# Two f tiles at a time on TensorE, and attention scores as 64x64 matmuls in its quadrants

## The chip, the cores and the metric

The kernel runs on one core of a Trainium2 chip. The metric is the device time of one execution in microseconds (us), as a median of several runs. Lower is better. TensorE multiplies matrices, VectorE (DVE), ScalarE (ACT) and GpSimd (POOL) work on elements, and SyncE (SP) issues the DMA transfers. PSUM is the memory that TensorE writes to.

## The reference

Local attention with block summaries, and then a feed-forward layer with a squared relu. There are 4 batches, 8 heads, 768 tokens and 64 channels per head. Each query sees the keys less than 16 positions away, and one summary key for each of 24 blocks of 32 tokens (the maximum over the block; the mean for the values).

```python
k_sum = k.reshape(B, H, nb, block, D).max(axis=3)
v_sum = v.reshape(B, H, nb, block, D).mean(axis=3)
scores_l = np.where(mask_l, scale * (q @ k.T), -1e9)       # |i - j| < 16
scores_s = scale * einsum('bhsd,bhnd->bhsn', q, k_sum) + log(block)
a = softmax(concatenate([scores_l, scores_s], axis=-1))
x = (a @ concatenate([v, v_sum], axis=2)).reshape(B * S, H * D)   # 3072 x 512
h = np.maximum(x @ w_in, 0.0)                              # 512 -> 2048
out = h * h @ w_out                                        # 2048 -> 512
```

All arrays are float32. The products are made of high and low parts, so each layer of the feed-forward part takes three products instead of one.

## The kernel before, in words

**Tiles.** The 3072 tokens are 24 query tiles g of 128 (t = g % 6 is a tile's place in its batch). A tile has two halves s of 64 queries; a half sees 96 keys of its window and 24 block keys, 120 columns in all (NK). Two tiles make a chunk c of 256 tokens, 12 chunks in all. The hidden 2048 columns are 16 f tiles of 128.

**Feed-forward, per chunk and f.** A row of the first layer (`ffn1`, L318) is 12 matmuls of 128x256 into a PSUM buffer `ph`, of which there are three in rotation. ACT then makes the relu `r` (L327) and the square `gh` (L334); DVE makes the exact square in `ph` (L339) and the rest `gl` (L343). The subtraction at L343 is the last reader of `ph` and sets its buffer free. A row of the second layer (`ffn2`, L359) is 6 matmuls of 128x512 which add to the two output buffers `o_ps` of the chunk. After f 15, `evict` copies both to SBUF on ACT (L106) and sends them out.

**Attention, per tile g.** `scores` (L222) makes 8 matmuls, one per head, into the two `s_ps` buffers of four heads each. The weights `q_sb` are 128x128: the two halves of the queries stand in two diagonal blocks of 64, and the other two blocks hold zeros, filled once by POOL (L103). `mask_max` (DVE, L234) and `exponentials` (ACT, L242) make the softmax, `inverse` and `norm` (DVE, POOL L257) divide, `turn` (L270) transposes 32x32 blocks on DVE, 12 instructions a tile, `outputs` (L283) makes 16 matmuls of 64 weight columns into `x_ps`, and `split_x` (L301, L304) splits the result into `xh` and `xl`, which `ffn1` reads. `place_k` copies the 24 block keys into `k_sb` with four copies of 64x96 on DVE (L157); for each batch after the first this is done for its first two tiles.

**The order of the work.** Every engine takes its instructions in the order in which the program records them. The start, chunks 0 and 1 and tiles 0 to 5, is a table written by hand (`START`): a token is one step, `F1.12` the first layer's row 12, `S4.1` the scores of half the heads of tile 4, `PK` the placing of the block keys. From chunk 2 on, `slot` records one f at a time: the first-layer row of f, the second-layer row of f - 2 (with the eviction after f 15), the attention's steps for this slot (`side`), relu to subtraction of f, and then what stands in `last` (scores, outputs, loads). `steps` gives each tile ten steps, and the loop at the end lays them over the slots of the chunk ahead: tile 2c + 2 is at step f + 2, tile 2c + 3 at step f - 6, tile 2c + 4 at step f - 14. So the outputs of one tile and the scores of the next but one come at the end of the same slot.

## Time and profile before

| what | value |
|---|---|
| median of 3 runs | 664.42 us (664.35 to 664.96) |
| profiled execution, its own time | 663.47 us |
| its span (first to last work on the core) | 661.7 us |
| TensorE busy | 633.0 us, 96% of the span |
| DVE, ACT, POOL busy | 404.9, 301.1, 110.6 us |
| granted TensorE clock, mean | 0.992 |
| moved by DMA | 61.87 MB, mean 94 GB/s |

The profile is one execution. A group's row shows the line, the engine, the operation, output <- inputs, the shape and the count; then the busy time, the mean ns of one, and the idle time ahead of it with what ended it. A timeline row shows start (us), length (us), engine, line and operation; `x2` joins two of a kind, and an idle time ahead of it stands in brackets. A row of busy time by stretches shows busy us of PE, PEld (weight loading), DVE, ACT and POOL with their counts, the granted clock, the DMA share and GB/s. A float32 matmul has two records in the trace. Starts of matmuls are measured, their lengths are modelled and overlap, so paces are read from start to start.

### The profile page before, as it was taken

Reading aid. Unit: us, or ns where it says so; the run is one execution under the profiler, and the core shown is the slowest. Engines: PE = TensorE matmul, PEld = TensorE weight load, DVE = VectorE, ACT = ScalarE, POOL = GpSimd, SP = SyncE. Lnnn points to the kernel's source line nnn. Section 1 sums busy time; section 2 is a strip of 40 time slices with the busy share of each in tenths; the row PEclk is TensorE's granted clock in tenths of the full one; section 3 lists DMA queues with packets and bytes.
Section 4 is the critical chain, followed back from the end, with each engine's and each line's share of the span. In section 5 each row is a group of like instructions: output and inputs, shape, how many; then the busy total and the mean of one; then the engine's idle time right before and its main releaser. Section 6 shows DMA issues by size and latency. Waiting matters only on the chain.

```text
span 661.7 us, 12338 instructions
## 1 busy us (share of the span) xinstructions
PE 633.0 (96%) x4668; PEld 566.5 (86%) x4668; DVE 404.9 (61%) x1247; ACT 301.1 (46%) x854; POOL 110.6 (17%) x87
## 2 busy tenths in 40 slices
PE   1788999999999999999999999999999999999997
PEld 1477999888889889999899998899898899988996
DVE  4678787656664684874863675865765645645332
ACT  2778867524424435335344344343444443443322
POOL 5464573401011011010010010010010110110000
PEclk9879999999999999999999999999999999999999
DMA  9999525005203314303103133212022020000000
GB/s 326 367 363 376 151 73 209 1 33 136 64 1 97 103 57 144 112 1 97 42 24 97 28 133 112 97 49 64 32 65 64 33 64 25 33 2 1 33 1 32
DMA packets 42314, 61.87 MB, mean 94 GB/s; under 512 B 27792, under 2 KB 27920, under 8 KB 40208
## 3 DMA queue, kind: packets, MB, share of 16 engines
q1 hardware_dynamic: 42256, 61.10, 28.3%
q8 instruction: 36, 0.59, 0.4%
q14 instruction: 22, 0.18, 0.1%
HBM read 54.80 MB, written 6.29 MB: 92 GB/s over the span
## 4 chain that ended last, share of the span: by engine, by line
PE 92%; DVE 3%; DMA 2%; ACT 1%; issue 1%; POOL 1%; SPq 0%; DVEq 0%; POOLq 0%; ACTq 0%
PE ph L318 41%; PE o_ps L359 39%; PE s_ps L222 7%; PE x_ps L283 3%; PE ph L263 1%; PE o_ps L129 1%; DMA kv<-in_kt 1%; DMA q_sb<-in_q 1%; DVE pT L270 1%; ACT e_sb L242 1%; DVE k_sb L157 0%; POOL e_sb L257 0%; DVE ksum L143 0%; POOL q_sb L103 0%; DVE ph L339 0%
## 5 line engine op out<-in xcount | busy, mean ns | idle before, releaser
L318 PE MATMUL ph<-xh,w_sb 128*128 128x256 f32 x1536 | 285.3, 284 | 0.7 <-ACT xh L301 0.7
L318 PEld LDWEIGHTS ph<-xh,w_sb 128*128 128x128 f32 x1536 | 248.3, 190 | 15.8 <-ACT xh L301 0.8
L359 PE MATMUL o_ps<-w_sb,gh 128*128 128x512 f32 x768 | 241.4, 395 | 0.0
L318 PE MATMUL ph<-xl,w_sb 128*128 128x256 f32 x768 | 217.0, 283 | 0.2 <-DVE xl L304 0.2
L339 DVE TENSOR_TENSOR ph<-ph,r 128x256 f32<-128x256 f32 x192 | 82.6, 431 | 157.1 <-ACT r L327 153.8
L327 ACT ACTIVATE r<-ph 128x256 f32<-128x256 f32 x179 | 68.2, 381 | 204.9 <-PE ph L318 203.7
L359 PE MATMUL o_ps<-w_sb,gl 128*128 128x512 f32 x384 | 151.3, 394 | 0.0
L318 PEld LDWEIGHTS ph<-xl,w_sb 128*128 128x128 f32 x768 | 145.5, 189 | 0.5 <-DVE xl L304 0.4
L359 PEld LDWEIGHTS o_ps<-w_sb,gh 128*128 128x128 f32 x768 | 131.1, 188 | 17.1
L257 POOL TENSOR_TENSOR e_sb<-e_sb,sm 128x480 f32<-128x480 f32 x42 | 41.7, 994 | 421.6 <-DVE nmx L234 360.9
L242 ACT ACTIVATE e_sb<-e_sb,nmx 128x120 f32<-128x120 f32 x192 | 73.9, 387 | 57.4 <-DVE nmx L234 57.4
L343 DVE TENSOR_TENSOR gl<-ph,gh 128x256 fp32r<-128x256 f32 x192 | 81.3, 424 | 29.7 <-ACT gh L334 7.1
L270 DVE STREAM_TRANSPOSE pT<-e_sb 32x256 f32<-32x256 f32 x216 | 94.2, 436 | 5.4 <-POOL e_sb L257 2.1
L334 ACT ACTIVATE gh<-r 128x256 fp32r<-128x256 f32 x192 | 80.4, 418 | 20.3 <-DVE r L329 7.7
L359 PEld LDWEIGHTS o_ps<-w_sb,gl 128*128 128x128 f32 x384 | 72.0, 188 | 17.1
L222 PE MATMUL s_ps<-k_sb,q_sb 128*128 128x120 f32 x384 | 51.4, 286 | 14.9 <-DVE k_sb L157 14.7
L222 PEld LDWEIGHTS s_ps<-k_sb,q_sb 128*128 128x128 f32 x384 | 46.9, 197 | 17.0 <-POOL w_sb L212 14.5
L234 DVE CUSTOM_DVE_ANT_0 e_sb<-s_ps,mask_sb 128x120 f32<-128x120 f32 x192 | 43.8, 274 | 5.3 <-PE ph L263 3.1
L205 POOL TENSOR_TENSOR w_raw<-w_raw 128x1024 int32<-128x1024 int32 x16 | 32.0, 2005 | 37.4 <-DVE w_raw L201 17.3
L242 ACT ACTIVATION_READ_ACCUMULATOR e_sb<-e_sb,nmx 128x1 f32 x192 | 36.1, 188 | 0.0
L283 PEld LDWEIGHTS x_ps<-pT,v_sb 128*64 128x64 f32 x768 | 24.4, 138 | 12.7 <-issue 9.5
L304 DVE TENSOR_TENSOR xl<-x_ps,xh 128x512 fp32r<-128x512 f32 x24 | 16.5, 688 | 27.0 <-ACT xh L301 27.0
(41 smaller groups left out, 293.0 us busy)
## 6 DMA issues: line engine op xcount, KB each, us to landing
w_raw<-in_w SPq DMA_DIRECT2D x16, 1024.0 KB, 10.7
k_sb<-in_k SPq DMA_DIRECT2D x24, 384.0 KB, 3.9
v_sb<-in_v SPq DMA_DIRECT2D x24, 384.0 KB, 3.7
kv<-in_kt SPq DMA_DIRECT2D x16, 384.0 KB, 5.3
q_sb<-in_q SPq DMA_DIRECT2D x48, 128.0 KB, 3.7
out<-ob SPq DMA_DIRECT2D x24, 256.0 KB, 2.0
kv<-in_vt SPq DMA_DIRECT2D x12, 384.0 KB, 4.9
vn<-in_v SPq DMA_DIRECT2D x2, 768.0 KB, 8.5
```

Source lines behind the costliest of these rows:

```text
L222: nc.tensor.matmul(s_ps[half][:, i, 0:NK], lhsT=q_sb[g % 2][:, h, :], rhs=k_sb[g % 2][:, :, h, :], start=True, stop=True)
L234: nc.vector.tensor_tensor_reduce(out=e_sb[:, h, 0:NK], in0=s_ps[half][:, i, 0:NK], in1=m, scale=-scale, scalar=3.0e38, op0=ALU.add, op1=AL ...
L242: nc.scalar.activation(e, e, AF.Exp, bias=nmx[half][:, i : i + 1], scale=-1.0, accum_out=sm[half][:, i : i + 1])
L257: eng.tensor_mul(out=e, in0=e, in1=sm[half].unsqueeze(2).to_broadcast([P, 4, NK]))
L270: nc.vector.transpose(out=pT[g % 2][j * 32 : j * 32 + 32, :, i * 32 : i * 32 + 32], in_=e_sb[i * 32 : i * 32 + 32, :, j * 32 : j * 32 + 32],)
L283: nc.tensor.matmul(xp[o : o + 64, h // 2, s * 64 : s * 64 + 64], lhsT=v_sb[g % 2][:, s, h * 64 : h * 64 + 64], rhs=pT[g % 2][:, h, s * 64 ...
L318: nc.tensor.matmul(ph, lhsT=w_sb[f][:, w, cc * P : (cc + 1) * P], rhs=x[c][:, cc, :], start=(n == 0), stop=(n == 3 * NC4 - 1))
L327: nc.scalar.activation(r, ph, AF.Relu)
L334: nc.scalar.activation(gh, r, AF.Square)
L339: nc.vector.tensor_mul(out=ph, in0=ph, in1=r)
L343: nc.vector.tensor_sub(out=gl, in0=ph, in1=gh.bitcast(F32))
L359: nc.tensor.matmul(o_ps[c][tt], lhsT=g_[:, ts_], rhs=w_sb[f][:, w, DM:], start=(first and n == 0), stop=(last and n == 2),)
```

## The change

- `slot` takes two f: two first-layer rows, the two second-layer rows that are waiting (with the eviction after f 15), the first half of the side work, relu to subtraction of the first f, the second half of the side work, and the same of the second f; then `last`.
- `steps` has 7 steps a tile instead of 10; the softmax is in one slot, the turns go by three. Tile 2c + 2 is at step i + 3 (i + 2 in chunk 2), tile 2c + 3 at step i - 1, tile 2c + 4 at step i - 5, where i is the number of the slot of two f. The scores of a tile come after slot 1 or 5, the outputs after slot 2 or 6.
- The scores are 4 matmuls of 64x64 weights for each of the four pairs of heads (r: head of the pair, which picks the rows; s: half of the queries, which picks the columns). `q_sb` holds no zeros any more, comes in one load instead of two, and the zero fills go. The two `s_ps` buffers become one tile of two banks, one for each r.
- `place_k` is one copy of 128x192 on DVE instead of four of 64x96.
- `xh`, `xl`, `gh` and `gl` lose the 8 spare columns (`SHIFT`); `gh` and `gl` have four buffers instead of three.
- The block sums of the next batch are loaded and made one pair of heads a tile (tiles 2 to 5), not two a tile (3 and 4).
- In `START`, `S5.1` stands some 20 tokens later, and `S6.0` behind `TT5.7`.

The core of the diff:

```diff
-SHIFT = 8
-BEHIND = 2
...
-F2.13 RE15v L:w13 SQ14 MU14 SQ15 MU15 F1.16 LO12a GL14v GL15v NR4.1 TT4.1 N4.1p S5.1 RE16a TT4.2 E4.1 TT4.3 MU16
+F2.13 RE15v L:w13 SQ14 MU14 SQ15 MU15 F1.16 LO12a GL14v GL15v NR4.1 TT4.1 N4.1p RE16a TT4.2 E4.1 TT4.3 MU16
+F1.17 SQ16 TT4.0 S5.1 E4.3 GL16v E4.2 SH12 S5.0 E4.0 RE17v AD12 F1.18 MU17 L:k7 NR4.0 L:v5 L:w15 F2.14 RE18a
...
     def load_q(g):
-        for s in range(2):
-            ps = slice(s * 64, s * 64 + 64)
-            nc.sync.dma_start(out=q_sb[g % 2][ps, :, ps], in_=q[g // NT, g % NT, ps])
+        nc.sync.dma_start(out=q_sb[g % 2], in_=q[g // NT, g % NT])
...
     def place_k(g):
-        dst = k_sb[g % 2].rearrange("a k (p two) j -> a k p two j", two=2)
-        for par in range(2):
-            for s in range(2):
-                nc.vector.tensor_copy(
-                    out=dst[s * 64 : s * 64 + 64, 4, :, par, :], in_=ksum[par * 64 : par * 64 + 64]
-                )
+        nc.vector.tensor_copy(out=k_sb[g % 2][:, 4], in_=ksum.unsqueeze(1).to_broadcast([P, 2, NPAIR, NB]))
...
-    def scores(g, half):
-        s_ps[half] = ps_s.tile([P, 4, P], F32, name="s_ps")
-        for i in range(4):
-            h = half * 4 + i
-            nc.tensor.matmul(
-                s_ps[half][:, i, 0:NK], lhsT=q_sb[g % 2][:, h, :], rhs=k_sb[g % 2][:, :, h, :], start=True, stop=True
-            )
+    def scores(g, p0, p1):
+        if g not in s_ps:
+            s_ps[g] = ps_s.tile([P, 2, NPAIR, P], F32, name="s_ps")
+        for p in range(p0, p1):
+            for r, s in ((0, 0), (1, 1), (0, 1), (1, 0)):
+                rs, ss = slice(r * 64, r * 64 + 64), slice(s * 64, s * 64 + 64)
+                nc.tensor.matmul(
+                    s_ps[g][ss, r, p, 0:NK], lhsT=q_sb[g % 2][rs, s, p, :], rhs=k_sb[g % 2][rs, :, s, p, :],
+                    start=True, stop=True,
+                )
...
     def high_square(r):
-        gh = shifted(CT, "gh", 3)
+        gh = work.tile([P, CT], F32R, name="gh", tag="gh", bufs=4)
...
     def slot(c, f, side, last):
-        ph = ffn1(c, f)
-        if len(behind) == BEHIND:
+        ph = [ffn1(c, f + i) for i in range(2)]
+        while behind:
             follow(*behind.pop(0))
-        for do in side:
-            do()
-        behind.append((c, f, *squares(ph), f == 0, f == NF - 1))
+        m = (len(side) + 1) // 2
+        for i in range(2):
+            for do in side[:m] if i == 0 else side[m:]:
+                do()
+            behind.append((c, f + i, *squares(ph[i]), f + i == 0, f + i == NF - 1))
         for do in last:
             do()
...
-        last[0] += [lambda: scores(g, 0), lambda: scores(g, 1)]
+        last[0].append(lambda: scores(g, 0, NPAIR))
...
-        side[1].append(lambda: softmax(g, 0, 2))
-        side[2].append(lambda: softmax(g, 2, 5))
-        side[3] += [lambda: inverse(0), lambda: norm(0, nc.gpsimd), lambda: softmax(g, 5, 8)]
-        side[4] += [lambda: inverse(1), lambda: norm(1, nc.gpsimd)]
-        for n in range(3):
-            side[5 + n].append(lambda n=n: turn(g, 4 * n, 4 * n + 4))
-        last[8].append(lambda: outputs(g))
+        side[1] += [lambda: softmax(g, 0, 5), lambda: softmax(g, 5, 8)]
+        for half in range(2):
+            side[2].append(lambda half=half: (inverse(half), norm(half, nc.gpsimd)))
+        for n in range(4):
+            side[3 + n // 2].append(lambda n=n: turn(g, 3 * n, 3 * n + 3))
+        last[5].append(lambda: outputs(g))
...
-            for f in range(NF):
+            for i in range(NF // 2):
                 side, last = [], []
-                at(side, last, 2 * c + 2, f + 2)
-                at(side, last, 2 * c + 3, f - 6)
-                at(side, last, 2 * c + 4, f - 14)
-                slot(c, f, side, last)
+                at(side, last, 2 * c + 2, i + (2 if c == 2 else 3))
+                at(side, last, 2 * c + 3, i - 1)
+                at(side, last, 2 * c + 4, i - 5)
+                slot(c, 2 * i, side, last)
```

How instructions move, at three places. First ACT where one chunk ends and chunk 5 begins, before. `r` and `gh` are relu and square, `ph` with a number is one first-layer row's buffer, `ob` is the copy of a finished output; `ph_3348` is f 0 of the new chunk, `ph_3382` f 1.

```order
L242 ACTIVATE e_sb_85,sm_3372<-e_sb_85,nmx_3371 128x120
L327 ACTIVATE r_3375<-ph_3348 128x256
L334 ACTIVATE gh_3377<-r_3375 128x256
L106 COPY ob_3401<-o_ps_2855 128x512
L106 COPY ob_3404<-o_ps_2856 128x512
L242 ACTIVATE e_sb_85,sm_3372<-e_sb_85,nmx_3371 128x120 x3
L327 ACTIVATE r_3416<-ph_3382 128x256
L334 ACTIVATE gh_3418<-r_3416 128x256
```

The same place on ACT in the changed kernel; `ph_3427` is f 0, `ph_3440` f 1, `ph_3367` and `ph_3380` are the last two f of the chunk before.

```order
L319 ACTIVATE r_3410<-ph_3367 128x256
L326 ACTIVATE gh_3412<-r_3410 128x256
L319 ACTIVATE r_3420<-ph_3380 128x256
L326 ACTIVATE gh_3422<-r_3420 128x256
L104 COPY ob_3465<-o_ps_2930 128x512
L104 COPY ob_3468<-o_ps_2931 128x512
L319 ACTIVATE r_3479<-ph_3427 128x256
L326 ACTIVATE gh_3481<-r_3479 128x256
L319 ACTIVATE r_3489<-ph_3440 128x256
```

The two copies stood between f 0 and f 1, and stand ahead of both now. On TensorE of the changed kernel, the fourth first-layer row of the chunk (f 3, the row after `ph_3496`) begins with a matmul that waits for DVE, and so do the scores that follow after the two second-layer rows:

```order
L310 MATMUL ph_3496<-xl_3116,w_sb_127 128x256
L310 MATMUL ph_3509<-xh_3114,w_sb_503 128x256 [waits DVE_49]
L310 MATMUL ph_3509<-xh_3114,w_sb_503 128x256
...
L351 MATMUL o_ps_3523<-w_sb_388,gh_3491 128x512 x2
L351 MATMUL o_ps_3523<-w_sb_388,gl_3494 128x512
L217 MATMUL s_ps_3557<-k_sb1_80,q_sb1_84 64x120 [waits DMAHW5_49,DMAHW6_49,DVE_49,PE_49]
L217 MATMUL s_ps_3557<-k_sb1_80,q_sb1_84 64x120 x15
L310 MATMUL ph_3576<-xh_3114,w_sb_201 128x256 x2
```

The scores are 16 instructions in one block here, and no outputs stand beside them. Last, DVE around the copy of the block keys for tile 13 (`k_sb1`), before: `pT0` are the turns of tile 12, the `L339` and `L343` rows multiply and subtract.

```order
L270 STREAM_TRANSPOSE pT0_86<-e_sb_85 32x8x32 x4
L339 TENSOR_TENSOR ph_3484<-ph_3484,r_3512 128x256
L343 TENSOR_TENSOR gl_3517<-ph_3484,gh_3514 128x256
L270 STREAM_TRANSPOSE pT0_86<-e_sb_85 32x8x32 x4
L339 TENSOR_TENSOR ph_3519<-ph_3519,r_3542 128x256
L343 TENSOR_TENSOR gl_3547<-ph_3519,gh_3544 128x256
L157 COPY k_sb1_80<-ksum_88 64x4x24 x4
L339 TENSOR_TENSOR ph_3549<-ph_3549,r_3572 128x256
```

And in the changed kernel, from f 0 of chunk 5 on (`L266` are the turns, `L331` and `L335` multiply and subtract, `L150` is the copy):

```order
L266 STREAM_TRANSPOSE pT0_86<-e_sb_85 32x8x32 x3
L331 TENSOR_TENSOR ph_3427<-ph_3427,r_3479 128x256
L335 TENSOR_TENSOR gl_3484<-ph_3427,gh_3481 128x256
L266 STREAM_TRANSPOSE pT0_86<-e_sb_85 32x8x32 x3
L331 TENSOR_TENSOR ph_3440<-ph_3440,r_3489 128x256
L335 TENSOR_TENSOR gl_3494<-ph_3440,gh_3491 128x256
L266 STREAM_TRANSPOSE pT0_86<-e_sb_85 32x8x32 x6
L331 TENSOR_TENSOR ph_3496<-ph_3496,r_3542 128x256
L335 TENSOR_TENSOR gl_3547<-ph_3496,gh_3544 128x256
L150 COPY k_sb1_80<-ksum_88 128x192
L331 TENSOR_TENSOR ph_3509<-ph_3509,r_3550 128x256
L335 TENSOR_TENSOR gl_3555<-ph_3509,gh_3552 128x256
```

All twelve turns and the squares of f 0 to f 2 now stand ahead of the copy within two slots of two f.

## The prediction

> **What bounds the kernel now.** I read the page first, for the share of each engine and the clock; then the busy time by stretches, for the part after the start; then the waits of TensorE; then the timeline around the places where the change moves work. The page's head, its busy line, the granted clock and the DMA row over the 40 slices:

> ```profile
> span 661.7 us, 12338 instructions
> PE 633.0 (96%) x4668; PEld 566.5 (86%) x4668; DVE 404.9 (61%) x1247; ACT 301.1 (46%) x854; POOL 110.6 (17%) x87
> ...
> PEclk9879999999999999999999999999999999999999
> DMA  9999525005203314303103133212022020000000
> ```

> TensorE is busy 96% of the span at nearly full clock. DMA is full only in the first four to five slices of 16.5 us. The stretch after the hand-ordered start:

> ```profile
> 180.00:650.00 470.00, 470.00 (x3484) 424.20 (x3483) 280.34 (x895) 190.35 (x595) 38.32 (x42) 1.00 0.18 57
> ```

> In these 470 us TensorE (the first pair of numbers) is busy for all 470.00 at a clock of 1.00: it waits for nobody. So there a us less of TensorE work is a us of time, and any wait that the change puts before TensorE is a us lost in full, since no slack is there to take it. The waits of TensorE over the whole span name one large one, which lies in the first 15 us:

> ```profile
> PE s_ps L222 <- DVE k_sb L157: 14.7, 2, 14.5
> ```

> This profiled execution took 663.47 us, the span 661.7 and 1.77 around it; the median of the three runs is 664.42 (664.35 to 664.96), so the profiled one is 0.95 below it. I sum against 663.47 and add 0.95 at the end. A difference of 0.2% (1.3 us) is about what a measurement of this kernel tells from none.

> **Pairing the f tiles.** The rows of the last chunk's start, at 615 us, give the paces and what I need further down:

> ```profile
> 615.20 1.29 ACT L106 COPY ob<-o_ps 128x512 f32<-128x512 f32 x2 [2.68 <-PE o_ps L359]
> 615.69 0.40 PE L318 MATMUL ph<-xh,w_sb 128*128 128x256 f32 x2
> ...
> 616.38 0.39 ACT L327 ACTIVATE r<-ph 128x256 f32<-128x256 f32 x1
> 616.80 0.42 ACT L334 ACTIVATE gh<-r 128x256 fp32r<-128x256 f32 x1
> 616.80 0.43 DVE L339 TENSOR_TENSOR ph<-ph,r 128x256 f32<-128x256 f32 x1 [3.71 <-ACT r L327]
> 617.11 0.63 PE L359 MATMUL o_ps<-w_sb,gh 128*128 128x512 f32 x2
> 617.36 0.42 DVE L343 TENSOR_TENSOR gl<-ph,gh 128x256 fp32r<-128x256 f32 x1
> 618.51 0.40 PE L318 MATMUL ph<-xh,w_sb 128*128 128x256 f32 x2
> ```

> A row of twelve first-layer matmuls takes 617.11 − 615.69 = 1.42 us (0.118 each), the six of the second 618.51 − 617.11 = 1.40 (0.233 each). Twelve times the spacing of two neighbours inside is the same 1.42: going from one layer to the other costs nothing now, so two rows of one and then two of the other gain nothing by themselves. Zero, and what TensorE does stays in number: 16 first and 16 second rows a chunk.

> **The scores.** Before, a tile's eight scores are full 128x128 matmuls (two passes each, 16 records), half of each weight being zeros. After, they are 16 64x64 matmuls, 32 records, four to a round. The price comes from two blocks in the timeline of TensorE, one of outputs followed by scores, one of outputs alone:

> ```profile
> 324.07 0.39 PE L359 MATMUL o_ps<-w_sb,gl 128*128 128x512 f32 x1
> 324.39 1.15 PE L283 MATMUL x_ps<-pT,v_sb 128*64 128x64 f32 x32
> 325.47 2.04 PE L222 MATMUL s_ps<-k_sb,q_sb 128*128 128x120 f32 x16
> ...
> 327.60 0.28 PE L318 MATMUL ph<-xl,w_sb 128*128 128x256 f32 x1
> ```
> ```profile
> 605.74 0.40 PE L359 MATMUL o_ps<-w_sb,gl 128*128 128x512 f32 x1
> 606.06 1.15 PE L283 MATMUL x_ps<-pT,v_sb 128*64 128x64 f32 x32
> ...
> 607.49 0.28 PE L318 MATMUL ph<-xl,w_sb 128*128 128x256 f32 x1
> ```

> From the last second-layer record to the third first-layer record it is 3.53 and 1.75 us; the same step without a block would be 0.233 + 2 × 0.118 = 0.47. So outputs with scores cost 3.06, outputs alone 1.28, and 16 score records 1.78, or 0.111 each for 120 columns. A 64-column output record should then take 0.059; 32 one after another would be 1.89, yet the block took 1.28. So the two column halves of the array do run at once: 16 pairs × 0.059 = 0.94, and 0.34 for going into and out of the split array. With four quadrants at once the scores would be 8 rounds × 0.111 + 0.34 = 1.23 instead of 1.78: −0.55, for the 17 tiles from 7 on −9.35. In the start, tiles 4, 5 and 6 go in two halves: 4 × 0.111 + 0.34 = 0.78 against 0.89, six times −0.105, −0.6. Together **−10.0**. That row halves also run at once no row shows. Bounds: without a switching cost −17, two at a time +7.8 (below).

> [...]

> **At a chunk's start: a new wait.** Now the copies of the finished chunk (2 × 0.65 us on ACT) stand behind the relu and square of the new chunk's f 0 and ahead of those of f 1. Afterwards the two last rows of the second layer come in one slot, and the copies stand ahead of relu and square of f 0. Behind them on ACT are both f of the slot. PSUM has three buffers for the first layer; the fourth row (f 3) needs the one of f 0, which the subtraction of f 0 on DVE sets free. The rows at 615 us show that very sequence, shifted by one f: a first-layer row starts at 615.69, right behind the chunk's last second-layer row; relu behind the copies at 616.38; subtraction until 617.36 + 0.42 = 617.78, that is 2.09 after 615.69. The fourth row is wanted 1.42 after 615.69, so TensorE stands 0.67 us, and a little for the signal. Ten boundaries (chunks 2 to 11) × 0.75 = **+7.5**; without the signal +6.7.

> **Placing the block keys: a second wait.** For tiles 7, 13 and 19 (second tile of a batch, in chunks 2, 5, 8) the copy of the block keys stands in slot 1 on DVE, behind turns of the tile before. The rows for its neighbours, and the ones of the place itself:

> ```profile
> 366.41 1.78 DVE L270 STREAM_TRANSPOSE pT<-e_sb 32x256 f32<-32x256 f32 x4 [0.29 <-POOL e_sb L257]
> 368.23 0.43 DVE L339 TENSOR_TENSOR ph<-ph,r 128x256 f32<-128x256 f32 x1
> 368.79 0.42 DVE L343 TENSOR_TENSOR gl<-ph,gh 128x256 fp32r<-128x256 f32 x1
> ```
> ```profile
> L157 DVE COPY k_sb<-ksum x32: 190/205/1743, 12.5 to 479.2; 64x96 f32<-64x96 f32 x32
> ```

> A turn is 1.78 / 4 = 0.445; multiplying and subtracting take 369.21 − 368.23 = 1.0. The new copy, 192 columns, lies between 0.2 (96 columns) and 0.43 (256 columns in the multiply); 0.3. Counted from the first-layer row of f 2: subtraction of f 0 ends at 2.1; three turns 3.4; f 1 4.4; six turns 7.1; f 2 8.1; copy 8.4, and the signal 8.5. TensorE has rows 2 and 3, the 0.75 of above and two second-layer rows, 1.42 × 2 + 0.75 + 2 × 1.40 = 6.4, and then wants scores. It stands 2.1 us, three times, in chunk 2 a little longer: **+6.5**. For even tiles the copy comes four slots later and no turns stand ahead of it: zero. In the kernel before, the copies have whole slots of cover: the waits show none of them after the start.

> **The start.** The chain that ended last, in its first pieces:

> ```profile
> 4.40 6.09 DMA kv<-in_kt
> ...
> 11.49 0.96 DVE ksum L143
> ...
> 12.48 1.74 DVE k_sb L157
> 14.23 0.21 DVE k_sb L157
> ...
> 14.54 3.67 PE s_ps L222 x16
> ...
> 18.22 5.74 DMA q_sb<-in_q
> ```

> Four copies, 12.48 to 14.44, become one of 0.2 to 1.74: up to −1.7, or nothing. The 3.67 us of scores become 8 rounds at the record pace there (0.229): −1.8. On the queue, q comes as 128 pieces of 2 KB instead of 1024 of 256 bytes, behind the same transfers: a gain with the sign known and no row for its size. Later steps of the start depend on weights that DMA brings at its limit, so part of it is lost again; bounds 0 and −3.5, I take the middle and a bit, **−2.2**. The two zero fills of q on POOL (1.85) lie beside DMA: zero. The signal of 14.44 to 14.54, 0.1, is the one used above.

> **Unpadded tiles.** The spare 8 columns behind the split activations and squares go. Prices of the readers:

> ```profile
> L318 PE MATMUL ph<-xh,w_sb 128*128 128x256 f32 x1536 | 285.3, 284 | 0.7 <-ACT xh L301 0.7
> L359 PE MATMUL o_ps<-w_sb,gh 128*128 128x512 f32 x768 | 241.4, 395 | 0.0
> L318 PE MATMUL ph<-xl,w_sb 128*128 128x256 f32 x768 | 217.0, 283 | 0.2 <-DVE xl L304 0.2
> L359 PE MATMUL o_ps<-w_sb,gl 128*128 128x512 f32 x384 | 151.3, 394 | 0.0
> ```

> Nothing in them tells padded from unpadded; different tiles of one kind differ by 1 ns. I take zero. 1 ns on 3456 records is 3.5 us either way, and 1% of the 192 first and 192 second rows, 192 × (1.42 + 1.40) = 541 us, is 5.4. Four instead of three buffers for the squares, fewer and larger loads and the softmax in one slot lie on engines that are 17 to 61% busy: zero, covered by two slots each.

> **Sum.** −10.0 − 2.2 + 7.5 + 6.5 = +1.8: 663.47 + 1.8 = 665.3, and on the median's footing 666.2.

> **The rivals.**
> *Two at a time* (0.11). Quadrants with the same rows might not overlap. Then 16 rounds: 16 × 0.111 + 0.34 = 2.12, +0.34 × 17 = +5.8; halves in the start 1.23 against 0.89, +2.0; the start gains 1.0 only: 664.42 + 7.8 − 1.0 + 14.0 = 685. The output rows speak against it, since there both column halves use all rows. All one after another (0.02) is 715. [...]
> *The other side: waits covered.* It is decided on DVE: if the turns wait for nothing and run before slot 1, the copy of the block keys is in time and TensorE never stands at the scores: 666.2 − 6.5 = 659.7 (0.13). If the buffer of f 0 also comes free in time, within 1.42 us of the row, all 14.0 go: 652 (0.07). For it: DVE is busy 280 of 470 us. Against it: engines keep their order, and the copies stood ahead of relu at 615 us.
> *Unpadded is slower* by 1%: 672 (0.12). *Unpadded is quicker* by 1 ns or more: 661 (0.09).

> **How the numbers follow.** My sum has 0.46, with its own range of ±4. The two outer cases, 652 and 685 or more (0.20), are left out: from 659.7 − 4 to 672 + 4, 656 to 676. Faster by over 0.2%: 0.09 of my own case, 0.12, 0.07, 0.07 = 0.35. Within: 0.13 of my own, the edges of others 0.05 = 0.18. Slower: the rest, 0.47.

> **What would show it.** Right: scores of a tile in 1.2 us of TensorE; TensorE idle some 14 us after 180 us, in ten pieces of 0.7 before the fourth row of a chunk, released by the subtraction, and three of 2 before scores, released by the block keys' copy; matmuls of 284 and 395 ns. Wrong: scores over 1.8, no idle time, or first-layer rows away from 1.42.

## The result, and the profile after

The changed kernel takes 655.64 us (median of 4 runs, 654.06 to 656.40), against 664.58 before: a ratio of 0.9862, with a 95% interval of 0.9843 to 0.9881. I had forecast 666.2, with a range of 656 to 676 and slower as the likelier side. The time lies just below the range, and the sign is wrong. The profiled execution, the fastest of the four, took 654.06.

The head of the page and the clock, after:

```profile
span 652.3 us, 13032 instructions
PE 608.9 (93%) x5052; PEld 535.2 (82%) x5052; DVE 402.2 (62%) x1223; ACT 295.4 (45%) x854; POOL 108.5 (17%) x85
...
PEclk9988999999999999999899999999999999999999
```

TensorE's busy time fell by 24.1 us (633.0 to 608.9), the span by only 9.4: TensorE now waits. First its busy time after the start, then who it waits for from 140 us on (us in all, times, longest):

```profile
180.00:640.00 460.00, 450.72 (x3717) 399.66 (x3717) 275.79 (x869) 184.18 (x587) 34.81 (x38) 1.00 0.18 58
```
```profile
PE ph L310 <- DVE gl L335: 5.9, 10, 0.6
PE s_ps L217 <- issue: 3.9, 2, 1.9
PE s_ps L217 <- DVE k_sb L150: 2.1, 1, 2.1
```

Both forecast waits are there: one at each of ten chunk starts, released by the subtraction, and three before scores. Two of these three are put down to "issue", which names no releaser; the rows below show the copy of the block keys ending 0.11 us before the scores start. This is chunk 5 on TensorE:

```profile
303.48 0.40 PE L310 MATMUL ph<-xh,w_sb 128*128 128x256 f32 x2
...
304.76 0.28 PE L310 MATMUL ph<-xl,w_sb 128*128 128x256 f32 x1
305.63 0.50 PE L310 MATMUL ph<-xh,w_sb 128*128 128x256 f32 x2 [0.60 <-DVE gl L335]
...
309.64 0.40 PE L351 MATMUL o_ps<-w_sb,gl 128*128 128x512 f32 x1
311.98 1.05 PE L217 MATMUL s_ps<-k_sb,q_sb 64*64 64x120 f32 x32 [1.94 <-issue]
312.96 0.55 PE L310 MATMUL ph<-xh,w_sb 128*128 128x256 f32 x2
```

And on ACT and DVE at the same place:

```profile
303.00 1.27 ACT L104 COPY ob<-o_ps 128x512 f32<-128x512 f32 x2 [6.72 <-PE o_ps L351]
304.17 0.39 ACT L319 ACTIVATE r<-ph 128x256 f32<-128x256 f32 x1
...
304.59 0.43 DVE L331 TENSOR_TENSOR ph<-ph,r 128x256 f32<-128x256 f32 x1 [5.11 <-ACT r L319]
305.15 0.42 DVE L335 TENSOR_TENSOR gl<-ph,gh 128x256 fp32r<-128x256 f32 x1
...
308.00 2.69 DVE L266 STREAM_TRANSPOSE pT<-e_sb 32x256 f32<-32x256 f32 x6
...
311.62 0.25 DVE L150 COPY k_sb<-ksum 128x192 f32<-128x192 f32 x1
```

Counted from the row of f 2 at 303.48, the subtraction of f 0 ends at 305.57 (2.09, as forecast), and the block keys' copy at 311.87 (8.39; forecast 8.4). The fourth row starts at 305.63 where 304.76 + 0.11 = 304.87 would do: 0.76 lost, and the profile calls 0.60 of it idle. The scores start 2.0 late.

What I had not foreseen shows in two first-layer rows in sequence without any wait, in the changed kernel:

```profile
326.92 0.40 PE L310 MATMUL ph<-xh,w_sb 128*128 128x256 f32 x2
...
329.66 0.62 PE L351 MATMUL o_ps<-w_sb,gh 128*128 128x512 f32 x2
...
332.41 0.40 PE L310 MATMUL ph<-xh,w_sb 128*128 128x256 f32 x2
```

Two first-layer rows take 2.74 us (2 × 1.42 = 2.84 before), two of the second 2.75 (2 × 1.40 = 2.80 before). The first five records of the pair still come every 0.118 us on average, all others every 0.113. The group means, 284 and 283 ns before, read 282 and 278:

```profile
L310 PE MATMUL ph<-xh,w_sb 128*128 128x256 f32 x1536 | 276.9, 282 | 6.6 <-DVE gl L335 5.9
...
L310 PE MATMUL ph<-xl,w_sb 128*128 128x256 f32 x768 | 213.7, 278 | 0.2 <-DVE xl L296 0.2
```

Two parts of the change are candidates: the missing spare columns, or two rows of a kind in sequence.

### The profile page after: what moved, and what is told of

It is laid out like the page before. It is cut to its first block, busy times and chain, and to the rows that moved or that the text cites. A ratio compares the mean times of both kernels' runs of the same rounds, so it can differ in the third digit from the quotient of the medians.

```text
span 652.3 us, 13032 instructions
## 1 busy us (share of the span) xinstructions
PE 608.9 (93%) x5052; PEld 535.2 (82%) x5052; DVE 402.2 (62%) x1223; ACT 295.4 (45%) x854; POOL 108.5 (17%) x85
## 4 chain that ended last, share of the span: by engine, by line
PE 90%; DVE 3%; ACT 2%; DMA 2%; issue 1%; SPq 0%; POOL 0%; DVEq 0%; POOLq 0%; ACTq 0%
PE ph L310 42%; PE o_ps L351 40%; PE x_ps L279 4%; PE s_ps L217 3%; DMA k_sb<-in_k 1%; DMA kv<-in_kt 1%; ACT e_sb L238 1%; PE ph L259 1%; DVE gl L335 1%; ACT w_raw L188 0%; ACT w_raw L184 0%; DVE pT L266 0%; DVE k_sb L150 0%; DVE sm L247 0%; SPq L134 0%
## 5 line engine op out<-in xcount | busy, mean ns | idle before, releaser
L310 PE MATMUL ph<-xh,w_sb 128*128 128x256 f32 x1536 | 276.9, 282 | 6.6 <-DVE gl L335 5.9
L310 PEld LDWEIGHTS ph<-xh,w_sb 128*128 128x128 f32 x1536 | 238.2, 189 | 18.7 <-DVE gl L335 7.9
L351 PE MATMUL o_ps<-w_sb,gh 128*128 128x512 f32 x768 | 238.6, 392 | 0.0
L310 PE MATMUL ph<-xl,w_sb 128*128 128x256 f32 x768 | 213.7, 278 | 0.2 <-DVE xl L296 0.2
L331 DVE TENSOR_TENSOR ph<-ph,r 128x256 f32<-128x256 f32 x192 | 82.3, 429 | 143.3 <-ACT r L319 140.4
L351 PEld LDWEIGHTS o_ps<-w_sb,gh 128*128 128x128 f32 x768 | 136.6, 188 | 24.2 <-ACT r L319 0.2
L335 DVE TENSOR_TENSOR gl<-ph,gh 128x256 fp32r<-128x256 f32 x192 | 81.3, 424 | 26.6 <-ACT gh L326 5.3
L266 DVE STREAM_TRANSPOSE pT<-e_sb 32x256 f32<-32x256 f32 x216 | 94.2, 436 | 4.7 <-POOL e_sb L253 0.7
L217 PE MATMUL s_ps<-k_sb,q_sb 64*64 64x120 f32 x768 | 27.3, 281 | 23.4 <-DVE k_sb L150 16.2
L217 PEld LDWEIGHTS s_ps<-k_sb,q_sb 64*64 64x64 f32 x768 | 21.2, 140 | 31.5 <-DVE k_sb L150 16.6
L104 ACT COPY ob<-o_ps 128x512 f32<-128x512 f32 x22 | 12.9, 588 | 66.2 <-PE o_ps L351 65.2
```

The costliest lines, as they stand in the source:

```text
L217: nc.tensor.matmul(s_ps[g][ss, r, p, 0:NK], lhsT=q_sb[g % 2][rs, s, p, :], rhs=k_sb[g % 2][rs, :, s, p, :], start=True, stop=True,)
L266: nc.vector.transpose(out=pT[g % 2][j * 32 : j * 32 + 32, :, i * 32 : i * 32 + 32], in_=e_sb[i * 32 : i * 32 + 32, :, j * 32 : j * 32 + 32],)
L310: nc.tensor.matmul(ph, lhsT=w_sb[f][:, w, cc * P : (cc + 1) * P], rhs=x[c][:, cc, :], start=(n == 0), stop=(n == 3 * NC4 - 1))
L331: nc.vector.tensor_mul(out=ph, in0=ph, in1=r)
L335: nc.vector.tensor_sub(out=gl, in0=ph, in1=gh.bitcast(F32))
L351: nc.tensor.matmul(o_ps[c][tt], lhsT=g_[:, ts_], rhs=w_sb[f][:, w, DM:], start=(first and n == 0), stop=(last and n == 2),)
```

## The experiments

The ratios are to the kernel before, in runs on the same chip. Differences in us between experiments sometimes cross chips; the kernel before has medians of 663.57 to 664.18 in the runs beside them.

### Spare columns or pairs: e1 and e2

The changed kernel with the spare columns put back:

```diff
-            x[c] = work.tile([P, NPAIR, CT], F32R, name=name, tag=name)
+            x[c] = shifted(NPAIR * CT, name, 2).rearrange("p (a b) -> p a b", b=CT)
...
-        gh = work.tile([P, CT], F32R, name="gh", tag="gh", bufs=4)
+        gh = shifted(CT, "gh", 4)
...
-        gl = work.tile([P, CT], F32R, name="gl", tag="gl", bufs=4)
+        gl = shifted(CT, "gl", 4)
```

> The changed kernel with the 8 spare columns put back behind xh, xl, gh and gl (four buffers for gh and gl), nothing else. In the changed kernel a first-layer record comes every 0.113 us instead of 0.118 and a second-layer record every 0.229 instead of 0.2325. Theory U (the spare columns made them slow): 0.118 and 0.2325 come back, 160 rows of each in the loop lose about 1.1 us a chunk, 10 to 13 us in all: 666 to 669 us. Theory P (two rows of a kind in sequence run faster than one): paces stay, 654 to 656 us.

Measured: 666.82 us (0.6 off my forecast of 666.2), ratio 1.0033 [1.0023, 1.0043]. The two rows of a kind, here:

```profile
333.45 0.40 PE L314 MATMUL ph<-xh,w_sb 128*128 128x256 f32 x2
...
336.28 0.62 PE L355 MATMUL o_ps<-w_sb,gh 128*128 128x512 f32 x2
...
339.06 0.40 PE L314 MATMUL ph<-xh,w_sb 128*128 128x256 f32 x2
```

2.83 and 2.78 us: close to the old paces (2.84 and 2.80), though the rows stand in pairs. The kernel before, without spare columns:

```diff
-SHIFT = 8
+SHIFT = 0
```

> The kernel before without the 8 spare columns, every instruction in its old place. Theory U: first-layer records every 0.113 us and second-layer ones every 0.229, 160 rows at 1.36 + 1.37 instead of 1.42 + 1.40 us, 651 to 654 us. Theory P: 0.118 and 0.2325 as before, 664 to 665 us.

Measured: 653.83 us, ratio 0.9854 [0.9835, 0.9872], with every instruction in its old place. One row of the first layer:

```profile
311.37 0.40 PE L318 MATMUL ph<-xh,w_sb 128*128 128x256 f32 x2
...
312.76 0.62 PE L359 MATMUL o_ps<-w_sb,gh 128*128 128x512 f32 x2
```

1.39 us, not 1.42. Theory U holds from both sides: the spare columns cost 11.2 us in the changed kernel and 10.2 in the one before (e10 shows below that the place of the buffers is behind it). Pairs add 2.1 us only without them: by the medians of rows that stand between rows of the other layer, a pair takes 2.746 us against 2 × 1.386, since the five slow records come once a pair, and 0.026 × 80 = 2.1. So this one edit alone did as well as the whole change.

### The copies at a chunk's start: e3

```diff
         if last:
+            done.append((c, f))
+
+    def evict_done():
+        for c, f in done:
             for tt in range(TPC):
                 evict(c, f, tt, nc.scalar)
+        done.clear()
...
             behind.append((c, f + i, *squares(ph[i]), f + i == 0, f + i == NF - 1))
+            if i == 1:
+                evict_done()
```

> The changed kernel with the two copies of a finished chunk recorded behind relu, square and subtraction of both f of the slot, not ahead of them. Theory B (the copies on ACT hold up the buffer that the fourth row needs, 0.76 us at each of ten chunk starts): those waits of TensorE go, -7.6 us, 647 to 649 us. Rival (the buffer is late for another reason, or the second layer's first row then waits for the output buffers instead): the idle time stays or moves, 654 to 657 us.

Measured: 639.60 us, ratio 0.9634 [0.9619, 0.9648]: 16.0 us less than the changed kernel. Theory B gave 7.6, so the time lies 7 us below its range. After 180 us TensorE waits for nothing, the output buffers included: it is busy for all 450.00 us from 180 to 630. Chunk 5, the relu of f 0, the copies of the finished chunk, the copy of the block keys and the scores:

```profile
296.85 0.38 ACT L319 ACTIVATE r<-ph 128x256 f32<-128x256 f32 x1 [3.30 <-PE ph L310]
...
300.27 1.27 ACT L104 COPY ob<-o_ps 128x512 f32<-128x512 f32 x2 [1.23 <-PE o_ps L351]
...
300.76 0.40 PE L310 MATMUL ph<-xh,w_sb 128*128 128x256 f32 x2
...
304.31 0.25 DVE L150 COPY k_sb<-ksum 128x192 f32<-128x192 f32 x1
...
306.35 1.05 PE L217 MATMUL s_ps<-k_sb,q_sb 64*64 64x120 f32 x32
```

The block keys are in place 3.8 us after the row of f 2, not 8.4. In the changed kernel the copies wait on ACT for the chunk's last second-layer row, the relu of f 0 stands behind them and starts 0.7 us after the row of f 2, and DVE sits idle for 5.11 us until that relu. Here the relu of f 0 starts 3.9 us ahead of the row of f 2, and the block keys come 4.6 us earlier by the same row. The second wait hung on the first. Only the scores of tile 7 still wait, 1.1 us. A chunk with no other wait takes 48.84 us against 49.73: a boundary cost 0.89, not 0.76, because the second record after the stop also comes 0.11 late.

### The block keys: e4, and both: e5

```diff
+        if b and t == 0:
+            side[0] += [lambda: place_k(g), lambda: place_k(g + 1)]
         if b and t < 2:
-            side[0].append(lambda: place_k(g))
...
         softmax(6, 0, 8)
+        place_k(7)
```

> The changed kernel with the block keys of both first tiles of a batch placed in one step, so the copy for tiles 13 and 19 stands a chunk earlier on DVE (tile 7: ahead of chunk 2). Theory K (DVE's queue holds up the scores by 2 us three times, and the clock is halved for 3.4 us after some of these stops, 1.8 us more each): -6 us without dips, -6 to -10 by what dips a run has: 646 to 650 us. Rival (the scores then wait for something else that is as late, the softmax or the loads): 653 to 656 us.

Measured: 648.17 us, ratio 0.9762 [0.9748, 0.9777], 7.5 less than the changed kernel. The stops before scores are gone, those at the boundaries stay (5.4 us in nine after 180 us). Theory K holds.

> The kernel with the copies behind the squares (639.6 us) and the block keys placed early as well. Theory K2 (late relu and square of f 0 also made the block keys late; with the copies moved, only one stop of 1.1 us before the scores of tile 7 is left): 638 to 639 us, the stop gone. Rival (the two waits are separate and both fixes add up in full, 7.6 and 7.5): 632 us.

Measured: 637.93 us, ratio 0.9609 [0.9594, 0.9623]. Theory K2 holds: the two fixes do not add up, this is 1.7 beyond e3. After 180 us TensorE does not wait at all, and this is the fastest kernel of the study:

```profile
180.00:630.00 450.00, 450.00 (x3735) 400.20 (x3735) 277.04 (x868) 188.45 (x589) 34.81 (x38) 1.00 0.18 59
```

### Which columns, and which place: e6 to e10, e13 to e18

e6 and e7 are e3 with the `shifted` lines of e1 for `gh` and `gl` alone, or for `xh` and `xl` alone. e8 has `SHIFT = 16` for all.

> The kernel with the copies behind the squares (639.6 us), with the 8 spare columns put back behind gh and gl alone. Theory X (the first layer is slow because its moving operand xh, xl is padded): first-layer records stay at 0.113, second-layer ones go to 0.232: 641 to 644 us. Theory G (padding of gh and gl is what slows all, since ACT and DVE write them while TensorE runs): both slow, 650 to 652 us.

Measured: 644.34 us, 4.7 above e3. Between rows of the other layer, two second-layer rows take 2.78 us and two first-layer rows 2.73. Theory X, though 0.3 above its range.

> The same base with the 8 spare columns behind xh and xl alone. Theory X: first-layer records at 0.118, second-layer ones stay at 0.229: 647 to 650 us. Theory G: nothing slows, 639 to 641 us.

Measured: 652.78 us, 13.2 above e3: 2.86 for two first-layer rows, but 2.80 for two of the second as well, whose operands have no spare columns here. So theory X fails on the second half. What `gh` and `gl` do have here is another address, since they lie behind `xh` and `xl`.

> The same base with 16 spare columns (64 bytes) behind all four instead of 8 (32 bytes). Theory A (a start off a 64-byte boundary costs): no loss, 639 to 641 us. Rival (the buffers standing a multiple of 1 KB apart is what is fast, and any spare columns break it): 650 to 652 us, as with 8.

Measured: 650.20 us, 10.6 above e3: theory A falls, its rival fits.

The next ones start from e5. e9 leaves 1 KB behind each `xh` buffer; e10 moves all work buffers by 32 bytes, and nothing else:

```diff
+    off = work.tile([P, 8], F32, name="off", tag="off", bufs=1)
+    nc.vector.memset(off, 0.0)
     nc.vector.memset(vsum, 0.0)
```

> The kernel with both fixes (637.9 us, no spare columns), with 256 spare columns (1 KB) behind each xh buffer, so that all later buffers move by a whole number of KB. Theory M (what matters is where xh, xl, gh and gl lie against each other within a KB: without spare columns all start at the same place of a KB): paces stay at 0.113 and 0.229, 637 to 639 us. Rival C (they must lie without gaps): first-layer records at 0.118, 646 to 650 us.

Measured: 638.78 us, paces as in e5. A gap of 1 KB does no harm.

> The kernel with both fixes, with one unused tile of 32 bytes ahead of all work buffers: xh, xl, gh and gl keep their distances to each other and move by 32 bytes against the weights and against a 64-byte boundary. Theory M (only their place against each other matters): 637 to 639 us, paces 0.113 and 0.229. Rival W (their place against the weights, or against a boundary, matters): 0.118 and 0.232, 647 to 652 us.

Measured: 652.05 us, 14.1 above e5, with no spare column anywhere. Theory M falls. Two first-layer rows behind scores take 2.94 us here:

```profile
335.42 0.50 PE L312 MATMUL ph<-xh,w_sb 128*128 128x256 f32 x2
...
338.36 0.62 PE L353 MATMUL o_ps<-w_sb,gh 128*128 128x512 f32 x2
```

The same stretch of the changed kernel takes 2.84 by the median. e13 to e15, e17 and e18 have 64, 128, 512, 256 and 480 bytes in that line; e16 puts the 32 bytes ahead of the constants, so the weights move along.

> The kernel with both fixes and 64 unused bytes ahead of all work buffers, where 32 bytes lost 14 us. Theory 64 (a 64-byte boundary decides): no loss, 637 to 639 us. Rival (a larger period, of 128 bytes to 1 KB, in the distance to the weights): first-layer records at 0.118 again, 648 to 653 us.

> The kernel with both fixes and 128 unused bytes ahead of all work buffers. Theory 128 (a period of 128 bytes decides): no loss, 637 to 639 us. Rival (a larger period): 648 to 653 us.

> The kernel with both fixes and 512 unused bytes ahead of all work buffers. Theory 512 (a period of 512 bytes or a divisor of it decides): no loss, 637 to 639 us. Rival (a period of 1 KB or more): 643 to 653 us.

> The kernel with both fixes and 32 unused bytes ahead of the constant tiles, so that weights and work buffers move together by 32 bytes and keep their distances. Theory W (the distance of the work buffers to the weights decides): no loss, 637 to 639 us. Rival B (an absolute boundary decides): 648 to 653 us, as with 32 bytes ahead of the work buffers alone.

> The kernel with both fixes and 256 unused bytes ahead of all work buffers. Theory 256 (the period of the distance to the weights is 256 bytes): no loss, 637 to 639 us. Rival 512 (the period is 512 bytes, the length of one 128-column slice): 643 to 653 us.

> The kernel with both fixes and 480 unused bytes ahead of all work buffers, which by a period of 512 is 32 bytes to the other side. Theory T (a fast stretch of distances that ends just above the present one): as fast, 637 to 639 us. Rival P (one fast place a period): 648 to 653 us.

Measured, in us; the rows are medians of the pairs that stand between rows of the other layer, with no scores or outputs beside them:

| work buffers moved by | time | two first-layer rows | two second-layer rows |
|---|---|---|---|
| 0 (e5) | 637.93 | 2.75 | 2.75 |
| 32 bytes (e10) | 652.05 | 2.84 | 2.80 |
| 64 (e13) | 651.05 | 2.87 | 2.75 |
| 128 (e14) | 651.40 | 2.83 | 2.80 |
| 256 (e17) | 639.46 | 2.75 | 2.75 |
| 480 (e18) | 651.67 | 2.82 | 2.80 |
| 512 (e15) | 638.68 | 2.75 | 2.75 |
| 32, weights too (e16) | 638.43 | 2.75 | 2.75 |

So neither the spare columns as such nor an address boundary decides, but the distance of the work buffers to the weights: in e10 and e16 the work buffers have the same addresses, and the weights stand 32 bytes apart. The constant tiles move with the weights in e16. These matmuls read only the weights of the two, so that it is the weights is likely, but not shown apart from the constants. The moves tried fit a period of 256 bytes, and the present place is the only one of a period, among those tried, at which both layers are fast; at 64 bytes the second layer is, too. Theories W, 512 (as a divisor of it) and 256 hold; 64, 128 and T fall.

### The scores: e11 and e12

Both start from e5. e11 takes the quadrants in the order of their rows, `((0, 0), (0, 1), (1, 0), (1, 1))`.

> The kernel with both fixes, with the four quadrants of a round in the order of their rows (both column halves of the upper rows, then both of the lower), not alternating. Theory Q (four quadrants run at once whatever their order): a tile's scores cost 1.2 us as before, 637 to 639 us. [...]

Measured: 638.89 us, ratio 0.9630 [0.9604, 0.9655], beside 0.9609 [0.9594, 0.9623] of e5; the block of scores is the same to the last hundredth:

```profile
305.26 1.05 PE L217 MATMUL s_ps<-k_sb,q_sb 64*64 64x120 f32 x32
306.24 0.51 PE L310 MATMUL ph<-xh,w_sb 128*128 128x256 f32 x2
```

0.98 us from the first score record to the next row, as in the alternating order (311.98 to 312.96 above). Theory Q holds. e12 takes full 128x128 matmuls; it leaves out the split by heads and halves, so its scores are other numbers:

```diff
-            for r, s in ((0, 0), (1, 1), (0, 1), (1, 0)):
...
+            for s in range(2):
                 nc.tensor.matmul(
...
+                    s_ps[g][:, s, p, 0:NK], lhsT=q_sb[g % 2].rearrange("k s p c -> k (s p c)")[:, p * P : p * P + P], rhs=k_sb[g % 2][:, :, s, p, :],
```

> The kernel with both fixes, with a tile's scores as eight full 128x128 matmuls of 120 columns, as many as in the kernel before, in the changed kernel's place. Both heads and halves run into each other in the products, so the scores are other numbers; the work of every engine but TensorE is the same. Theory S (16 score records at 0.111 us in place of 1.19 us with the switch): +0.59 on each of the 17 tiles from 7 on, and up to +2 in the start: 648 to 650 us. [...]

Measured: 651.80 us, 13.9 above e5 and 1.8 above theory S's range. The block of scores:

```profile
284.89 1.94 PE L216 MATMUL s_ps<-k_sb,q_sb 128*128 128x120 f32 x16
286.60 0.49 PE L309 MATMUL ph<-xh,w_sb 128*128 128x256 f32 x2
```

1.71 us, and the way in is 0.23 (284.66 to 284.89), without the 0.33 that the quadrants' block has. A chunk with two tiles' scores takes 50.05 us against 48.84: 0.605 a tile, 10.3 for 17. The loop starts 1.7 later too. That is the 11.8 by which the profiled execution lies above e5's; the rest of the 13.9 lies within the spread of this kernel's runs (649.72 to 653.06).

## Why the prediction was wrong, point by point

**What bounds it, and the waits that come in.** Right. A us of TensorE work was a us of time (e12: 10.3 us of longer scores and a loop that starts 1.7 later, 11.8 more in the profiled execution), and so was a wait. The boundary wait was priced at 0.75 and cost 0.89, ten times: 8.9 for 7.5. The wait for the block keys was priced at 6.5 for three tiles; e4 gives 7.5, the three stops and one stretch of half clock (below). I treated the two as separate terms, which their sum allowed; e3 shows that the first causes most of the second: without it the stops of tiles 13 and 19 are gone.

**The scores.** Right: −0.55 a tile forecast, −0.605 by e12. The split of the price was off, and its errors cancel: a block costs the neighbouring rows 0.095 us going in and as much going out (2.843 and 2.842 us for a pair of rows beside a block, 2.748 and 2.746 without, in e5), 0.19 and not 0.34, and a round takes 0.98 / 8 = 0.123 and not 0.111. That row halves run at once as column halves do, which no row had shown, is shown by 0.98 us for 32 records, which two at a time would take 1.78 by my record pace (16 × 0.111). The rival "two at a time" is out, by the rows and by e11. In either order of the quadrants a block takes 0.98 us, so neighbours on the same rows cost nothing more here.

**The start.** −2.8 forecast with the scores' halves. In the profiled executions the loop's first row came at 149.98 before, 146.06 after and 149.22 in e1, so without the new paces the start gained 0.8. These are one execution each, and the start varies: in e3, e4 and e5, whose hand-ordered start is that of the changed kernel, the row came at 146.80, 147.94 and 146.48. The chain that I priced (keys' copy, first scores) is shorter: the first scores start at 14.06 us instead of 14.54 and take 1.88 instead of 3.67. The queries come sooner, too: 256 KB land 2.9 us after their issue, by the median of 24 loads, where 128 KB took 3.7 in the 48 loads before. Yet TensorE waits later in the start for DMA (3.5 us) and ACT (2.8). The term seems too large; its size stays open.

**Unpadded tiles: the step that failed.** I wrote "Nothing in them tells padded from unpadded; different tiles of one kind differ by 1 ns. I take zero." They were worth 11.2 us (e1 against the changed kernel), and without that term my sum was within 0.6 us of the kernel it described. That closeness is in part luck: the start gained less than priced and the two waits cost 2.4 us more, while scores and pairs took 1.8 us more off. Two things were wrong with the bound. It was taken from mean lengths, which the profile models, and not from the spacing of starts, where a record of the first layer loses 0.005 us and one of the second 0.004; the 1% that I allowed for a row was 2.4% and 1.5% (e2: 1.386 for 1.420 and 1.374 for 1.395). And the rows compared were padded against padded; that tells nothing of a step to another place. What the term stands for is that place: 32 bytes of distance cost 14.1 us with no spare column anywhere (e10), and nothing when the weights move along (e16). I had the rival "unpadded is quicker", at 0.09 and with 661 us, so the way was seen as possible, and its size was half of the measured one.

**Pairing the f tiles.** Forecast zero; 2.1 us by e2, and only where the fast place is kept (e1: 2.829 against 2 × 1.420, 0.9 us).

**The ledger.** Of the 9.4 us of span: start −3.9; scores −10.3; boundaries +8.9; block keys +7.5; the pace of the rows, 49.73 us a chunk against 50.76 in e1, −10.3 in ten chunks; and pairs, which e1 has as well, −0.9. Together −9.0; the other 0.4 is not traced.

## What to carry to other kernels

A bound for an edit that only moves buffers is not zero because the instructions stay: where TensorE never waits, measure it alone, since 0.005 us on thousands of matmuls was worth as much here as the planned gain. When an order is changed, walk each queue for what stands ahead of the step that frees a buffer; the fix is often one move in the order (e3), and a second stall may be the first one's echo. Read paces from start to start, not from the mean length.

## What the runs showed of the hardware that was not expected

A stop of 2 us can cost more than its length. Behind the stop in chunk 5 the changed kernel ran at half clock for 3.4 us, by the stretches there (the third number from the end is the granted clock):

```profile
312.00:314.00 2.00, 2.00 (x38) 1.84 (x39) 1.55 (x11) 0.53 (x3) 0.00 (x0) 0.82 0.04 8
314.00:316.00 2.00, 2.00 (x11) 2.00 (x11) 0.19 (x2) 1.80 (x9) 0.00 (x0) 0.50 0.70 160
```

It cost 1.5 us: chunk 5 lost 3.6 where chunk 8, with the same stop and no such stretch, lost 2.1. No other such stretch lies between 75 and 651 us, so one of three stops of 1.9 to 2.1 us was followed by one. DMA was busy behind the other two stops too (0.48 to 0.59 of its time) at a clock of 1.00. None of the ten stops of 0.6 us was followed by such a stretch.
